# Block queries, keys and values in step-major scratch: one load each per step, input rows as 128 runs, two buffers shared

## The chip, the cores and the metric

The kernel runs on one core of a Trainium2 chip. A core has a matmul engine (TensorE, PE in the profile, with its weight loads as PEld), a vector engine (VectorE, DVE), a scalar engine (ScalarE, ACT), GpSimd (POOL) and a queue processor for transfers (SyncE, SP). Transfers are issued from the queues of SP, ACT and POOL and are carried out by 16 DMA engines that all queues share. The metric is the device time of one execution in microseconds (us). The kernel before took 2215.84 us, the median of three executions that lie between 2213.84 and 2217.09 us.

## The reference, cut to what matters

Two independent results are concatenated. The first (`A`) is a convolution over 2048 rows done by a Fourier transform. The second (`B`) is a recurrence over 64 segments, and most of the time goes there:

```python
# B: x (2048, 1024), 32 heads of 128, M = 8 memory rows, seg = 32
mem = mem0
for s in range(64):
    h = concatenate([mem, x[32 * s : 32 * s + 32]])        # 40 rows
    q, k, v = (einsum('td,dhe->hte', h, W) for W in (Wq, Wk, Wv))
    p = softmax(where(mask, q @ k.T * 128 ** -0.5, -1e9))  # a row sees the memory and earlier rows
    o = einsum('hte,hed->td', p @ v, Wo)
    mem = o[:8]
    outs.append(o[8:])
# A: outa = q * (causal_convolution(shift(k) * v, ssm_k) + ssm_D * shift(k) * v)
```

Each weight matrix is 1024 x 4096 in bf16, 8 MB. Four of them don't fit in the core's memory, so part of the weights is loaded again in every step.

## The kernel before, in words

**Stages.** Up to about 448 us the kernel computes `A` and, in between, prepares `B`. From then on it runs the recurrence, one step for each segment (`for s in range(n_seg)`, line 908), and after the last step it projects what was put aside, about 61 us.

**What is prepared.** Of the 40 rows of a step, the 8 memory rows and the first 24 rows of x go through the step's own projections. The last 8 rows of each segment, the *block rows*, depend on no memory: their queries, keys and values are computed for all 64 segments ahead of the recurrence, by the object `Rows` (lines 125 to 190). It works through 12 units, one for each projection (q, k, v) and group g of 8 heads, in the order q0 k0 v0 q1 k1 v1 v2 v3 q2 k2 q3 k3. Matmuls of such a unit stand between those of `A`; the accumulators are copied by ACT (from q3 on by ACT and DVE in turn) to the buffer `stq` (tile `st`, 128 x 64 x 128, queries and keys of a group) or `stv` (tile `sv`, 128 x 4 x 1024, values). Each of these has one buffer. When a group is complete, the whole tile is written to the scratch `QKBd` (line 184, after k0, k1, k2 and k3) or `VBd` (line 187, after v0 to v3), both from POOL's queue. The next unit of the kind can't write the buffer before that transfer has read it.

**A step.** It has four groups of 8 heads. For each group: the projections of queries and keys (`qk_part`, line 749), their copy to `qks` (`qk_out`, ACT), the value projection (`v_part`, 764) with its copy (`v_out`, ACT), transposes of `qks` (`tr_a`, PE) and copies of the result and of the block keys to QT and KT (DVE, 785 to 787). The scores, the softmax and the product with the values of group g are done among the projections of the next groups (`scores`, `softmax`, `pv`). After the fourth group come the output projections `wo` of all groups into Y, with the last softmax and products among them; ACT copies Y to `Y_sb` (961), PE transposes it, and DVE writes the memory rows into the next step's `hT` (`fill_mem`, 889). The next step's projections need that.

**Transfers of a step.** SP streams 17 pairs of weight tiles (512 KB each) through a ring of 5 buffers (`place`, 712): a load is issued when PE has finished with the ring slot. Between them SP issues four loads `qkb<-QKBd` (793), one for each group, each 128 rows of 256 bytes, into two buffers. POOL issues, at the end of a step, one store of block outputs (`OLd`, 856), four loads of the block values `VB` (798, 16 KB each) and four stores of the step's output from `Y_sb` (967). ACT issues one load of the next step's rows, `H` (661), at the start of group 2; `H` and `Y_sb` share one buffer (tag "st"), so this load waits for the four stores of the step before. `H` is transposed in `h_rows` (880) among the output projections.

**Order.** Instructions run on every engine in the order in which the program writes them. A wait of one instruction, a DMA issue too, holds everything behind it on the same queue. Transfers signal through a fixed set of semaphores, eight for those of SP and ACT together and eight for those of POOL, taken in turn: the ninth waits until the first has landed. So four stores, four loads and one store of a step on POOL's queue are one more than the eight.

**Names and lines of the steps to come:** `QKBd` 184 and 793, `VBd` 187 and 798, `load_h` 661, `h_rows` 880, `Y_sb` 961 and 967, `PT` (the transposed softmax, DVE, 834), the final loads of 512-byte rows 941.

## Time and profile before

| | us |
|---|---|
| median of three executions | 2215.84 |
| span of the profiled execution, first to last instruction | 2198.5 |
| median less span: what lies around the span (the page gives the profiled execution no other time of its own) | 17.3 |
| PE busy | 1808.6 (82%) |
| DVE busy | 1082.4 (49%) |
| ACT busy | 836.0 (38%) |
| POOL busy | 500.4 (23%) |
| first and last copy of Y to `Y_sb`: starts | 448.0 and 2137.0 |

A profile page gives busy times by engine, a picture of the span in 40 slices, the DMA queues with the packets that they moved (q1 is SP's, q10 ACT's, q0 POOL's, q8 fetches instructions), the chain of waits that ended last, and groups of instructions with what they waited for. The trace below it holds every packet with its size and its time on a DMA engine. The 64 copies to `Y_sb` mark the steps: 63 steps lie between 448.0 and 2137.0 us, 26.81 us each.

### The profile page before, as it was taken

Reading aid. Unit: us, or ns where it says so; the run is one execution under the profiler, and the core shown is the slowest. Engines: PE = TensorE matmul, PEld = TensorE weight load, DVE = VectorE, ACT = ScalarE, POOL = GpSimd, SP = SyncE. Lnnn points to the kernel's source line nnn. Section 1 sums busy time; section 2 is a strip of 40 time slices with the busy share of each in tenths; the row PEclk is TensorE's granted clock in tenths of the full one; section 3 lists DMA queues with packets and bytes.
Section 4 is the critical chain, followed back from the end, with each engine's and each line's share of the span. In section 5 each row is a group of like instructions: output and inputs, shape, how many; then the busy total and the mean of one; then the engine's idle time right before and its main releaser. Section 6 shows DMA issues by size and latency. Waiting matters only on the chain.

```text
span 2198.5 us, 88235 instructions
## 1 busy us (share of the span) xinstructions
PE 1808.6 (82%) x37779; PEld 1028.8 (47%) x37808; DVE 1082.4 (49%) x3235; ACT 836.0 (38%) x2538; POOL 500.4 (23%) x983
## 2 busy tenths in 40 slices
PE   4788877688888888788888878888888888888878
PEld 2332233354444445444544545544444445444558
DVE  6896822244544444444445445544444444444530
ACT  5456721133333334333333334333333333333320
POOL 4004622022222222222222222222222222222210
PEclk9999999899999999999999999999999999999999
DMA  7799889699999999999999999999999999999990
GB/s 255 267 353 350 302 302 369 248 354 345 343 341 365 344 358 367 339 342 333 349 352 361 365 357 364 364 345 353 358 353 347 349 347 361 323 348 345 357 328 21
DMA packets 275666, 732.29 MB, mean 333 GB/s; under 512 B 73323, under 2 KB 84539, under 8 KB 274761
## 3 DMA queue, kind: packets, MB, share of 16 engines
q1 hardware_dynamic: 242062, 683.06, 85.8%
q0 software_dynamic: 24320, 37.37, 5.2%
q10 hardware_dynamic: 8892, 6.23, 0.9%
q8 instruction: 295, 4.83, 0.9%
q14 instruction: 97, 0.79, 0.1%
HBM read 676.14 MB, written 59.18 MB: 334 GB/s over the span
## 4 chain that ended last, share of the span: by engine, by line
DMA 38%; PE 33%; issue 8%; DVE 3%; ACT 2%; POOL 1%; ACTq 1%; SPq 0%; POOLq 0%; DVEq 0%
PE qkacc L749 10%; DMA wring<-Wstv 10%; DMA wring<-Wstqk 8%; DMA wring<-Wsto 7%; PE yacc L863 6%; DMA out_dram<-Y_sb 5%; PE vacc L764 5%; DMA OLd<-OL 5%; PE otacc L846 3%; PE pl L979 3%; PE tp L777 2%; ACT OT L851 1%; PE otacc L848 1%; PE S L805 1%; DVE S L820 1%
## 5 line engine op out<-in xcount | busy, mean ns | idle before, releaser
L749 PE MATMUL qkacc<-Wqk,hT 128*32 128x512 bf16 x4096 | 354.6, 388 | 1.3 <-issue 1.3
L851 ACT CAST OT<-otacc 128x80 bf16<-128x80 f32 x1024 | 183.4, 233 | 438.6 <-PE otacc L848 391.2
L854 POOL COPY OL<-OT 128x64 bf16<-128x64 bf16 x252 | 63.3, 251 | 1221.9 <-ACT OT L851 1221.9
L764 PEld LDWEIGHTS <-hT 128*32 128x32 bf16 x8192 | 227.4, 98 | 190.1 <-issue 140.4
L749 PEld LDWEIGHTS <-hT 128*32 128x32 bf16 x8192 | 179.0, 98 | 215.4 <-issue 79.7
L863 PE MATMUL yacc<-Wo,OT 128*32 128x256 bf16 x5632 | 248.6, 278 | 22.2 <-issue 21.8
L863 PEld LDWEIGHTS <-OT 128*32 128x32 bf16 x8192 | 188.0, 97 | 103.5 <-issue 74.1
L764 PE MATMUL vacc<-Wv,hT 128*32 128x256 bf16 x5120 | 229.9, 279 | 2.7 <-issue 1.4
L749 PE MATMUL qkacc<-wring,hT 128*32 128x512 bf16 x2048 | 210.1, 398 | 24.3 <-DMA wring<-Wstqk 22.4
L764 PE MATMUL vacc<-wring,hT 128*32 128x256 bf16 x3072 | 145.4, 278 | 92.6 <-DMA wring<-Wstv 89.3
L846 PE MATMUL otacc<-PT,vsb 32*128 32x64 bf16 x2048 | 147.9, 192 | 55.3 <-ACT OT L851 49.1
L786 DVE COPY QT<-tp 128x256 bf16<-128x256 bf16 x256 | 74.7, 292 | 206.4 <-PE tp L777 198.8
L749 PE MATMUL qkacc<-Wearly,hT 128*32 128x512 bf16 x2048 | 171.0, 413 | 3.7 <-DVE hT L881 0.4
L718 ACT COPY wring<-park 128x1024 bf16<-128x1024 bf16 x128 | 129.9, 1015 | 110.4 <-PE qkacc L749 98.4
L755 ACT CAST qks<-qkacc 128x512 bf16<-128x512 f32 x256 | 150.5, 588 | 53.8 <-PE qkacc L749 48.6
L830 DVE TENSOR_REDUCE sm<-P 128x4 f32<-128x256 bf16 x256 | 107.6, 420 | 118.9 <-ACT P L828 118.9
L772 ACT CAST vsb<-vacc 128x256 bf16<-128x256 f32 x256 | 95.4, 373 | 179.2 <-PE vacc L764 178.2
L827 ACT ACTIVATE P<-S 128x128 bf16<-128x128 f32 x256 | 71.5, 279 | 238.3 <-DVE P L826 123.4
L819 DVE TENSOR_REDUCE mx<-S 128x4 f32<-128x160 f32 x256 | 83.2, 325 | 155.8 <-PE S L816 154.3
L863 PE MATMUL yacc<-wring,OT 128*32 128x256 bf16 x2520 | 131.5, 278 | 32.5 <-DMA wring<-Wsto 20.2
L798 POOL DMA_DIRECT2D VB<-VBd x256 | 152.3, 600 | 8.9 <-issue 3.6
L848 PE MATMUL otacc<-PT,VB 32*128 32x64 bf16 x2048 | 144.3, 188 | 8.9 <-issue 8.7
(218 smaller groups left out, 2830.0 us busy)
## 6 DMA issues: line engine op xcount, KB each, us to landing
wring<-Wstqk SPq DMA_DIRECT2D x448, 512.0 KB, 6.3
wring<-Wstv SPq DMA_DIRECT2D x320, 512.0 KB, 6.2
wring<-Wsto SPq DMA_DIRECT2D x315, 512.0 KB, 6.2
SK<-s_sb SPq DMA_DIRECT2D x8, 1024.0 KB
SU<-s_sb SPq DMA_DIRECT2D x8, 1024.0 KB, 5.4
QKBd<-stq POOLq DMA_DIRECT2D x4, 2048.0 KB, 9.8
Kg<-SK SPq DMA_DIRECT2D x16, 512.0 KB, 6.0
Ug<-SU SPq DMA_DIRECT2D x16, 512.0 KB, 8.0
```

The lines of the kernel that those rows point to most:

```text
L718: nc.scalar.copy(t[:, 0, :], park[key][0][:])
L749: nc.tensor.matmul(u.qk[p0:p0 + 32, :], lhsT=hT[:, kc, :], rhs=w[t][:, c2 * 512:(c2 + 1) * 512], start=(kc == 0), stop=(kc == 7), tile_pos ...
L755: nc.scalar.copy(u.qks[:], u.qk[:])
L764: nc.tensor.matmul(u.vacc[32 * c:32 * c + 32, 0:256], lhsT=hT[:, kc, :], rhs=w[kc % 2][:, c * 256:(c + 1) * 256], start=(kc == 0), stop=(k ...
L772: nc.scalar.copy(u.v[:], u.vacc[:, 0:256])
L798: nc.gpsimd.dma_start(VB[32 * c:32 * c + 32, :], VBd[8 * s:8 * s + 8].rearrange("r (g c x) -> c g r x", g=4, c=4)[c])
L819: nc.vector.tensor_reduce(out=mx[:], in_=S[:], op=ALU.max, axis=AX.X)
L830: nc.vector.tensor_reduce(out=sm[:], in_=P[:], op=ALU.add, axis=AX.X)
L846: nc.tensor.matmul(o, lhsT=u.v[r, i * 128:(i + 1) * 128], rhs=PTv[r, i, 0], start=True, stop=False, tile_position=(32 * c, 0))
L848: nc.tensor.matmul(o, lhsT=VB[r, i * 128:(i + 1) * 128], rhs=PTv[r, i, 1], start=False, stop=True, tile_position=(32 * c, 0))
L851: nc.scalar.copy(u.OT[:, 2 * c:2 * c + 2, :], ov[:, :, 0:40])
L863: nc.tensor.matmul(Y[32 * dq:32 * dq + 32, 0:256], lhsT=u.OT[:, hh, 0:32], rhs=w[hh % 2][:, dq * 256:(dq + 1) * 256], start=(u.g == 0 and ...
```

## The change

- The scratch `QKBd` is laid out by step: for a step, 128 rows of 4 groups x 128 values. A step loads it whole, 128 rows of 1 KB, in one transfer into one buffer, after the scores of the last group; `tr_a` and `scores` read slices of it. The price of the layout is on the writing side: a group's write has 128 x 64 runs of 256 bytes instead of 128 runs of 16 KB. It is issued from ACT's queue instead of POOL's.
- The scratch `VBd` is laid out so that a step's block values are one contiguous piece of 64 KB. One transfer loads it instead of four. A group's write is 16 transfers of 64 KB (runs of 512 bytes) on POOL's queue instead of one.
- The next step's input rows `H` are loaded as 128 rows of 512 bytes in the order of memory (partition = row x 4 + quarter), where the load before had the quarter outermost (4 x 32 x 512 bytes); `h_rows` reads its transposes in the new order. The first `H` takes two transfers instead of eight.
- `H` now shares its buffer with `qks`, and `Y_sb` with `PT`. The load of `H` is issued after the fourth group instead of before the third, `h_rows` stands after the last output projection, and the load of `VB` stands behind the four stores of `Y_sb`.

```diff
-    QKBd = dram.tile([4, 128, n_seg, 128], BF, name="QKBd")
+    QKBd = dram.tile([n_seg, 128, 4, 128], BF, name="QKBd")
-    VBd = dram.tile([n_seg * 8, 4096], BF, name="VBd")
+    VBd = dram.tile([n_seg, 4, 4, 8, 256], BF, name="VBd")
...
-                        nc.gpsimd.dma_start(QKBd[g].rearrange("e s x -> e (s x)"),
-                                            self.st[:].rearrange("e s h t r -> e (s h t r)"))
+                        nc.scalar.dma_start(QKBd[:, :, g, :].rearrange("s e x -> e s x"),
+                                            self.st[:].rearrange("e s h t r -> e s (h t r)"))
                     if m == "v" and j == 7:
-                        nc.gpsimd.dma_start(VBd.rearrange("(rb p) n -> p rb n", p=128)[:, :, g * 1024:(g + 1) * 1024],
-                                            self.sv[:])
+                        for rb_ in range(4):
+                            for c in range(4):
+                                nc.gpsimd.dma_start(VBd[16 * rb_:16 * rb_ + 16, c, g],
+                                                    self.sv[:, rb_, c * 256:(c + 1) * 256])
...
-        H_ = act.tile([128, 256], BF, tag="st", name="H")
+        H_ = act.tile([128, 256], BF, tag="qks", name="H")
...
-            nc.scalar.dma_start(H_[:], xq[:, 32 * s - 8:32 * s + 24, :])
+            nc.scalar.dma_start(H_[:], x[32 * s - 8:32 * s + 24].rearrange("t (dq c) -> (t dq) c", dq=4))
...
-    def load_b(s, g):
-        u = G()
-        u.g = g
-        u.qkb = act2.tile([128, 128], BF, tag="qkb", name="qkb")
-        nc.sync.dma_start(u.qkb[:], QKBd[g][:, s, :])
+    def load_b(s):
+        qkb = act.tile([128, 4, 128], BF, tag="qkb", name="qkb")
+        nc.sync.dma_start(qkb[:], QKBd[s])
+        return qkb
...
     def load_vb(s):
-        for c in range(4):
-            nc.gpsimd.dma_start(VB[32 * c:32 * c + 32, :],
-                                VBd[8 * s:8 * s + 8].rearrange("r (g c x) -> c g r x", g=4, c=4)[c])
+        nc.gpsimd.dma_start(VB[:], VBd[s].rearrange("c g r x -> (c g r) x"))
...
         for g in range(4):
-            if g == 2 and s + 1 < n_seg:
-                H = load_h(s + 1)
...
-            if g < 3:
-                nxt = load_b(s, g + 1)
-            elif s + 1 < n_seg:
-                nxt = load_b(s + 1, 0)
...
             v_out(u)
+            if g == 3 and s + 1 < n_seg:
+                H = load_h(s + 1)
...
-        softmax(us[3], scores(us[3]))
+        S = scores(us[3])
+        if s + 1 < n_seg:
+            qkb = load_b(s + 1)
+        softmax(us[3], S)
...
         wo(us[1], Y, range(4, 8))
+        wo(us[2], Y)
+        pv(us[3], s, (0, 1))
+        pv(us[3], s, (2, 3), True)
+        wo(us[3], Y)
         if s + 1 < n_seg:
             hT = new_hT()
             h_rows(H, hT, 8)
-        wo(us[2], Y)
-        pv(us[3], s, (0, 1))
-        pv(us[3], s, (2, 3), True)
-        if s + 1 < n_seg:
-            load_vb(s + 1)
-        wo(us[3], Y)
-        Y_sb = act.tile([128, 256], BF, tag="st", name="Y_sb")
+        Y_sb = act.tile([128, 256], BF, tag="PT", name="Y_sb")
...
         for dq in range(4):
             nc.gpsimd.dma_start(outb[32 * s:32 * s + 24, dq * 256:(dq + 1) * 256], Y_sb[32 * dq + 8:32 * dq + 32, :])
+        if s + 1 < n_seg:
+            load_vb(s + 1)
```

More of the change, by code (lines that the diff above doesn't have):

```diff
@@ L652, in load_h @@
     def load_h(s):
-        H_ = act.tile([128, 256], BF, tag="st", name="H")
-        xq = x.rearrange("t (dq c) -> dq t c", dq=4)
+        H_ = act.tile([128, 256], BF, tag="qks", name="H")
         if s == 0:
-            for dq in range(4):
-                nc.gpsimd.dma_start(H_[32 * dq:32 * dq + 8, :], mem0[:, dq * 256:(dq + 1) * 256])
-                nc.gpsimd.dma_start(H_[32 * dq + 8:32 * dq + 32, :], xq[dq, 0:24, :])
+            nc.gpsimd.dma_start(H_[0:32, :], mem0.rearrange("t (dq c) -> (t dq) c", dq=4))
+            nc.gpsimd.dma_start(H_[32:128, :], x[0:24].rearrange("t (dq c) -> (t dq) c", dq=4))
         else:
-            nc.scalar.dma_start(H_[:], xq[:, 32 * s - 8:32 * s + 24, :])
+            nc.scalar.dma_start(H_[:], x[32 * s - 8:32 * s + 24].rearrange("t (dq c) -> (t dq) c", dq=4))
         return H_
@@ L882, in h_rows @@
             hT_[:].rearrange("p (dq hf) t -> p dq hf t", hf=2)[:, :, :, r0:32],
-            tp[:, 0:256].rearrange("p (hf dq r) -> p dq hf r", hf=2, dq=4)[:, :, :, r0:32])
+            tp[:, 0:256].rearrange("p (hf r dq) -> p dq hf r", hf=2, dq=4)[:, :, :, r0:32])
     def fill_mem(hT_, Ysrc):
@@ L898, in fused_kernel @@
     load_vb(0)
-    nxt = load_b(0, 0)
+    qkb = load_b(0)
     for key in resident:
@@ L915, in fused_kernel @@
                     res[key] = res[at]
-            u = nxt
+            u = new_u(g)
             us.append(u)
```

6 lines of the change are left out of this document (4 added, 2 removed).

## The prediction

> **What bounds the kernel now.** I read the page first, then the stages by windows, then the waits inside the recurrence, then the places of the preparation that the change touches.
>
> ```profile
> PE 1808.6 (82%) x37779; PEld 1028.8 (47%) x37808; DVE 1082.4 (49%) x3235; ACT 836.0 (38%) x2538; POOL 500.4 (23%) x983
> DMA  7799889699999999999999999999999999999990
> q1 hardware_dynamic: 242062, 683.06, 85.8%
> q0 software_dynamic: 24320, 37.37, 5.2%
> q10 hardware_dynamic: 8892, 6.23, 0.9%
> ```
>
> The DMA row stands at 9 in nearly every slice, and SP's queue alone holds 85.8% of the time of 16 engines. The windows (columns: busy time of PE, PEld, DVE, ACT, POOL, granted clock, DMA share, GB/s) say where that is so:
>
> ```profile
> 187.00:250.00 63.00, 57.17 (x318) 17.86 (x321) 54.42 (x93) 48.83 (x92) 39.14 (x39) 1.00 1.00 356
> 250.00:285.00 35.00, 31.14 (x160) 9.56 (x163) 29.34 (x49) 25.89 (x49) 25.00 (x25) 1.00 0.66 228
> 361.00:373.00 12.00, 2.97 (x16) 1.30 (x15) 1.92 (x2) 0.59 (x1) 1.00 (x2) 0.78 0.98 394
> 385.00:402.00 17.00, 16.95 (x86) 7.95 (x85) 3.46 (x5) 2.85 (x5) 0.00 (x0) 1.00 0.35 125
> 402.00:414.00 12.00, 6.80 (x136) 3.55 (x135) 5.09 (x14) 5.09 (x9) 2.92 (x5) 1.00 0.48 182
> 600.00:2000.00 1400.00, 1173.78 (x28825) 687.83 (x28818) 672.65 (x2300) 525.17 (x1833) 313.73 (x681) 0.97 0.98 351
> ```
>
> In the recurrence (the last row) the DMA engines are full (0.98; 0.975 by the sum of the packets) and PE is not (1174 of 1400). Transfers bind it, and a step of 26.81 us has about 0.65 us of DMA idleness. The preparation changes its limit: PE with DVE and ACT in lockstep at 250 to 285, transfers at 361 to 373, PE at 385 to 402, and a single transfer at 402 to 414. What causes the idleness in the recurrence is in the waits there (total us, times, longest):
>
> ```profile
> SPq L793 <- DMA H<-in_B_x_dram: 86.1, 38, 5.1
> ACT OT L851 <- DMA out_dram<-Y_sb: 32.6, 10, 4.5
> POOL out_dram L967 <- DMA OLd<-OL: 53.4, 46, 3.1
> ```
>
> They are one string. POOL's ninth transfer of the step, the fourth output store, waits for the first (`OLd`). The load of `H` waits on ACT's queue for that store, because they share a buffer, and holds the copies behind it. SP's `qkb` load waits for `H`, whose semaphore it takes over, and the weight loads stand behind SP's `qkb`.
>
> **The change in the recurrence.** The trace's packet records give prices by size: 18.3 ns for 256 bytes (26,880 of them between 600 and 2000 us, all `qkb`), 29.3 ns for the 512-byte rows of `H`, 48.3 ns for 1 KB, 177 ns for 4 KB, 9.4 ns for a semaphore.
>
> - `qkb`: 4 x 128 x 18.3 / 16 = 0.586 us of every engine per step, against 128 x 48.3 / 16 = 0.386 (the 1 KB price is that of POOL's output stores). Three transfers fewer on SP, three on POOL: 6 x 9.4 ns. Sum -0.25 us a step, on the engines that bind: 63 x 0.25 = -16 us.
> - `VB`: the records show four packets of 4 KB for each 16 KB load, 16 a step; the single load moves the same bytes, so nothing but the semaphores. It saves POOL 3 x 0.58 us of issuing, on an engine with 314 of 1400 us busy. It now stands behind the four stores: Y's copy + 0.4, stores 4 x 0.52, own issue 0.6, landing 5.3, so about 8.4 us after the copy. The first user (the products of group 0, in group 2) comes about 11 us after it: hidden.
> - `H`: same bytes, but in the records (four steps after 1000 us) its 128 packets are never more than five at a time and take 2.0 to 4.8 us: about four of the sixteen engines carry it, 0.94 us each, instead of 0.23 on all. Spread evenly, the four lose 0.7 us a step. It is issued after the fourth group and needs 3.0 to 5.3 us; `h_rows` comes about 9 us later (1060 to 1069 us in one step of the chain). The transposes then run while ACT copies Y (0.37 us against 0.33): hidden.
> - The string of waits goes: six transfers on POOL's queue instead of nine, and `H` waits only for transposes just done. What is late next is `PT`: DVE's first transpose of a step must wait for the stores from `Y_sb`. In the trace it starts 7.9 to 10.8 us (median 9.3) after Y's copy; the last store would land at 0.4 + 3 x 0.52 + 5.1 = 7.1 us (longest 9.0). Mostly in time. If late, DVE's copies of QT and KT queue behind it and PE waits for these; the ring's lead covers part.
> - SP's `qkb` waits for the scores of group 3; the weight load behind it waits for a projection that PE does later anyway, so it holds up nothing. It is needed after the next `hT` (1061 to 1070 us in that step), against 5.2 us to land.
>
> How much of the 0.65 us of idleness goes is bounded by 0 (PE's own waits cause it) and 0.65 (41 us in all). The string costs SP 1.7 us a step, the uneven `H` 0.7 us on four engines; I take 0.3 us, just under half, -19 us. **Recurrence: -35 us**, between -16 and -57.
>
> **The change in the preparation.** No store of 256-byte runs is in the trace. Its nearest row is the 256-byte load, 18.3 ns; from below it can't be cheaper than its bytes at the 16 KB price (640 ns per 16 KB, 10 ns per 256 bytes); from above I take twice the load's, 36.6 ns, a row that is read before it is written. I take 18.3, since the prices above grow evenly with size whatever the kind: 8192 x 18.3 / 16 = 9.4 us per write against 128 x 640 / 16 = 5.1. The places where the writes stand, from the timeline of POOL, the waits of ACT, the chain, and the timeline of SP at the end (start, length):
>
> ```profile
> 187.18 0.56 POOL L184 DMA_DIRECT2D QKBd<-stq  x1
> 236.32 0.80 POOL L187 DMA_DIRECT2D VBd<-stv  x1 [0.38 <-ACT stv L149]
> 238.19 1.17 POOL L572 TENSOR_TENSOR Yre<-pa,pb 128x512 bf16<-128x512 bf16 x1
> ACT stq L149 <- DMA QKBd<-stq: 12.2, 1, 12.2
> 404.45 8.49 DMA QKBd<-stq
> 2120.89 11.58 SPq L941 DMA_DIRECT2D Wearly<-OLd  x2
> 2122.16 10.32 SPq L941 DMA_DIRECT2D Wearly<-OLd  x1
> ```
>
> - Writes after k0 (113 us) and k1 (187 us): +4.3 us of DMA each in full stretches, but loads run two sets ahead and 250 to 285 has DMA to spare. The issue moves from POOL to ACT, which at 187 us is in lockstep with PE (49 of 63 us busy), so what the issue takes there is lost. Of the final 512-byte loads, two on SP, the first (4096 runs) issues in 1.3 us, the second stands 10.3 us. For 8192 runs I take 3 us, ends 0.6 and 10. Sum +4 (0 to 13).
> - v0's 16 stores: POOL is idle. v1's at 236 us: 16 x 0.55 to 0.8 us, plus waits for semaphores, 10 us in which POOL's `Yre` and `Yim` are held up; PE uses them about 3 us later, so +7; ACT's copy to `stv` waits until the last lands, 236.3 + 10 + 5.3 = 251.6 against 242.8, 8.8 us, the same time over. +8 (5 to 12). v2's fall where POOL is free from 287 to 307. v3's at 316 us hold the stores of `A`'s output by 10 us; DVE waits for these stores already, but transfers bind there: +3 (0 to 9).
> - After k2 (361 us): the next unit's copy already waits 12.2 us for this write, and PE with it; 4.3 us more reach the end, since PE binds at 385 to 402: +4.5 (0 to 14).
> - After k3: the chain stands 2.37 us before POOL's issue and 8.49 for the landing (413.07). From ACT at 402.2: 1 + 9.4 + 1.2 gives 414: +1 (0 to 10). SP's `qkb` now waits for this write, but SP's loads of Wo behind it already did.
>
> **Preparation: +20.5 us.** Moving the write from POOL takes nothing off a path; its cover, idle POOL time, is exchanged for ACT's.
>
> **Sum.** Span 2198.5 - 35 + 20.5 = 2184; with the 17.3 us around it, 2201.3. The profiled execution's whole time isn't shown; I add the median's rest.
>
> **A rule against the change.** The Trainium skill's page "DMA: Bandwidth & Descriptors", section Specifications, puts line rate at 512 bytes and up and says that below it a DMA reads, modifies and writes. By that the 256-byte runs, harmless as loads, would cost double as stores, which is the rival "dear stores" below. No store of this trace can show it. The same page (section "Why a DMA increments its semaphore by 16 and not by 1") derives the number of engines from the outermost sizes; for `H` before, 4 and 128, that gives four, and the five at most in flight agree.
>
> **The rivals.**
>
> - *Dear stores*: each 256-byte run 36.6 ns. k2's and k3's writes add 9.4 us each to the path, the first two about 6 together: 2201 + 24.5 = 2226, slower. It decides from about 29 ns on: 24.5 us for 18.3 ns is 1.34 us per ns, and 10.8 ns more use up the gain of 14.5. For it: nothing in the trace writes short runs, and the steps of 128 KB between a partition's runs are new. Against: loads grow smoothly down to 256 bytes.
> - *ACT held by its own issue*, as SP's second load was: 10 us instead of 3 at 187 us, some 5 at 113: about 2213, no change. For: 512 runs an engine, twice what SP had queued in the first load. Against: the first load itself was taken at once.
> - *Idleness stays*: PE's waits, not the string, empty the queues: -16 + 20.5, 2220, slightly slower. For: SP waits more for PE (226 us on `qkacc`) than for `H`.
> - *All idleness goes*: -57 + 20.5, 2179.
>
> **How the numbers follow.** My forecast 0.45 (own range 2188 to 2211); all idleness 0.08; ACT held 0.12; idleness stays 0.13; dear stores 0.22. A change under 0.2% (4.4 us) can't be told from none here. Faster 0.45 + 0.08 = 0.53; same 0.12; slower 0.13 + 0.22 = 0.35. The range leaves out the edge of the best case and the worst of dear stores with a held ACT: 2176 to 2242.
>
> **What would show it.** Steps (63 between first and last copy of Y) near 26.25 us, with neither SP waiting for `H` nor ACT for `Y_sb`'s stores; the first copy of Y near 468 us instead of 448; 256-byte stores near 18 ns and four writes on q10. Wrong if ACT's issue at about 190 us lasts over 5 us, if k2's or k3's write takes 15 us or more, or if DVE's `PT` waits for the stores in many steps.

## The result, and the profile after

The changed kernel took 2188.57 us (median of 13 executions, 2183.43 to 2202.34). The kernel before, run beside it on the same chips, took 2210.56 (13 executions). The ratio is 0.9921, with a 95% interval of 0.9899 to 0.9943: 0.8% faster, where 2201 us and "faster" with a chance of 0.53 were forecast. The profiled spans, 2198.5 and 2186.4 us, differ by 12.1. The profiled execution of the kernel before lies below its median: in the 13 executions of the changed kernel the time is 1.8 to 2.4 us above the span, so by an estimate from these it took about 2200.6 us, 10 us less than the median of 2210.56. The profile doesn't show where the other executions spend these 10 us; if it is in the recurrence, a step of theirs is 0.16 us longer than the table's 26.81.

That net figure hides two larger ones. The first and the last copy of Y to `Y_sb` divide the span into preparation, recurrence and end:

| | before, us | after, us | difference | forecast |
|---|---|---|---|---|
| first copy of Y (preparation) | 447.96 | 486.67 | +38.7 | +20.5 |
| 63 steps between first and last copy | 1689.0 | 1638.4 | -50.6 | -35 |
| one step | 26.81 | 26.01 | -0.80 | -0.56 |
| from the last copy to the end of the span | 61.5 | 61.3 | -0.2 | 0 |
| span | 2198.5 | 2186.4 | -12.1 | -14.5 |

Both halves are larger than forecast by nearly the same amount (18 us and 16 us), so the sum came out nearly right although its two terms did not: that is luck.

The page of the changed kernel: busy time by engine, the DMA row in 40 slices, and the queues (packets, MB, share of 16 engines' time).

```profile
PE 1791.2 (82%) x37808; PEld 1023.5 (47%) x37808; DVE 1093.1 (50%) x3235; ACT 836.3 (38%) x2538; POOL 405.5 (19%) x841
DMA  7798969789999999999999999999999999999990
q1 hardware_dynamic: 214414, 683.05, 84.9%
q0 software_dynamic: 18368, 28.88, 4.0%
q10 hardware_dynamic: 42480, 14.62, 2.7%
```

The writes of block queries and keys now show as 42,480 packets on ACT's queue (q10, 8,892 before). SP's packets fall by 27,648: 384 rows and three transfers' semaphores on 16 engines fewer in each of 64 steps. POOL's busy time falls by 95 us. The DMA row still stands at 9 through the recurrence: the bound has not moved. The window over the recurrence (columns: busy time of PE, PEld, DVE, ACT, POOL, granted clock, DMA share, GB/s) shows the same:

```profile
600.00:2000.00 1400.00, 1185.83 (x29773) 703.17 (x29769) 706.64 (x2383) 543.43 (x1897) 222.85 (x541) 0.98 0.98 362
```

In the same 1400 us the engines carry 362 GB/s, where it was 351. What SP waits for inside the recurrence (us in total, times, longest):

```profile
SPq L712 <- PE qkacc L749: 318.3, 323, 3.9
SPq L712 <- DMA wring<-Wstqk: 250.0, 264, 4.1
SPq L712 <- PE yacc L865: 147.5, 142, 3.0
...
SPq L791 <- PE yacc L865: 59.7, 48, 3.1
```

The wait of 86.1 us for `H` is gone, as is ACT's wait for the output stores. SP waits instead for PE to free a ring slot (318 us, 226 before): the loads now arrive at the ring before PE is done with it. The load of the block queries and keys (line 791) waits for PE 48 times, and that was expected.

In the preparation the new writes stand out. The tile `QKBd` (issue min/median/max in ns, then the engines that waited for it):

```profile
L184 ACTq DMA_DIRECT2D QKBd<-stq x4: 366/372/389, 112.1 to 439.5; - x4
...
  ACT stq L149: 16.6, 1
  DVE stq L151: 11.0, 1
```

and the two waits of SP's queue in the windows from 105 to 150 us and from 197 to 230 us:

```profile
SPq L112 <- DMA QKBd<-stq: 12.5, 1, 12.5
...
SPq L520 <- DMA QKBd<-stq: 10.1, 1, 10.1
```

ACT issues such a write in 0.37 us, so ACT is not held by its issue. But the write lands late (a median of 16.5 us from issue to landing, 9.8 when the runs were 16 KB), and SP, which takes its semaphores from the same eight as ACT, twice stands behind it for over 10 us in the middle of `A`.

### The profile page after: what moved, and what is told of

Read it like the earlier page. It is cut to its first block, busy times and chain, and to the rows that moved or that the text cites. A ratio compares the mean times of both kernels' runs of the same rounds, so it can differ in the third digit from the quotient of the medians.

```text
span 2186.4 us, 88021 instructions
## 1 busy us (share of the span) xinstructions
PE 1791.2 (82%) x37808; PEld 1023.5 (47%) x37808; DVE 1093.1 (50%) x3235; ACT 836.3 (38%) x2538; POOL 405.5 (19%) x841
## 3 DMA queue, kind: packets, MB, share of 16 engines
q10 hardware_dynamic: 42480, 14.62, 2.7%
## 4 chain that ended last, share of the span: by engine, by line
PE 45%; DMA 34%; DVE 8%; issue 7%; ACT 5%; POOL 1%; SPq 0%; ACTq 0%; DVEq 0%; POOLq 0%
PE qkacc L749 13%; DMA wring<-Wstv 13%; DMA wring<-Wstqk 10%; PE yacc L865 8%; PE vacc L764 5%; PE otacc L848 3%; PE pl L980 3%; DMA wring<-Wsto 2%; DMA QKBd<-stq 2%; PE tp L777 2%; PE ps_k L176 1%; PE S L807 1%; DVE S L822 1%; DVE mx L821 1%; PE ps_q L176 1%
## 5 line engine op out<-in xcount | busy, mean ns | idle before, releaser
L764 PEld LDWEIGHTS <-hT 128*32 128x32 bf16 x8192 | 220.2, 97 | 181.5 <-issue 103.3
L749 PEld LDWEIGHTS <-hT 128*32 128x32 bf16 x8192 | 178.1, 97 | 216.4 <-issue 77.0
L865 PEld LDWEIGHTS <-OT 128*32 128x32 bf16 x8192 | 194.6, 97 | 84.9 <-issue 61.4
L850 PE MATMUL otacc<-PT,VB 32*128 32x64 bf16 x2048 | 141.4, 188 | 10.8 <-issue 10.8
L966 POOL DMA_DIRECT2D out_dram<-Y_sb x256 | 129.2, 511 | 38.1 <-ACT Y_sb L960 35.0
## 6 DMA issues: line engine op xcount, KB each, us to landing
QKBd<-stq ACTq DMA_DIRECT2D x4, 2048.0 KB, 16.5
```

The costliest lines, as they stand in the source:

```text
L749: nc.tensor.matmul(u.qk[p0:p0 + 32, :], lhsT=hT[:, kc, :], rhs=w[t][:, c2 * 512:(c2 + 1) * 512], start=(kc == 0), stop=(kc == 7), tile_pos ...
L764: nc.tensor.matmul(u.vacc[32 * c:32 * c + 32, 0:256], lhsT=hT[:, kc, :], rhs=w[kc % 2][:, c * 256:(c + 1) * 256], start=(kc == 0), stop=(k ...
L850: nc.tensor.matmul(o, lhsT=VB[r, i * 128:(i + 1) * 128], rhs=PTv[r, i, 1], start=False, stop=True, tile_position=(32 * c, 0))
L865: nc.tensor.matmul(Y[32 * dq:32 * dq + 32, 0:256], lhsT=u.OT[:, hh, 0:32], rhs=w[hh % 2][:, dq * 256:(dq + 1) * 256], start=(u.g == 0 and ...
L966: nc.gpsimd.dma_start(outb[32 * s:32 * s + 24, dq * 256:(dq + 1) * 256], Y_sb[32 * dq + 8:32 * dq + 32, :])
```

## The experiments

The questions: which part of the change shortens the step, which part lengthens the preparation, and whether the three supposed mechanisms (the string of waits, the short runs, the uneven `H`) are the ones at work. "Step" below is the distance between the first and the last copy of Y divided by 63; "idle" and "work" are the parts of it in which the DMA engines stood still or moved packets (from the packet records); "4 KB" is the mean time of a weight packet. "First Y" is the length of the preparation. The kernel before of each ratio ran beside it. Each step comes from one profiled execution, and the executions of one kernel differ by up to 28 us (four_2pool, 2198.75 to 2226.71), which is 0.44 us a step if all of it lies in the recurrence; so differences of a few hundredths of a us say nothing by themselves, and larger ones are trusted where the medians agree.

| kernel | median, us | ratio, 95% interval | first Y | step | idle | work | 4 KB, ns |
|---|---|---|---|---|---|---|---|
| before | 2210.56 | | 448.0 | 26.81 | 0.65 | 26.16 | 176.9 |
| after | 2188.57 | 0.9921 (0.9899 to 0.9943) | 486.7 | 26.01 | 0.45 | 25.55 | 174.5 |
| h_late | 2167.13 | 0.9797 (0.9741 to 0.9852) | 447.4 | 26.31 | 0.38 | 25.93 | 174.9 |
| one_load | 2161.70 | 0.9828 (0.9757 to 0.9900) | 451.0 | 26.08 | 0.23 | 25.85 | 174.8 |
| h_quarter | 2186.61 | 0.9889 (0.9833 to 0.9945) | 483.1 | 26.04 | 0.36 | 25.68 | 175.1 |
| four_vb | 2189.66 | 0.9918 (0.9886 to 0.9949) | 483.1 | 26.06 | 0.48 | 25.57 | 174.1 |
| four_loads | 2258.86 | 1.0214 (1.0151 to 1.0277) | 487.3 | 27.25 | 0.92 | 26.33 | 178.9 |
| qkb_write | 2225.87 | 1.0110 (1.0046 to 1.0174) | 465.5 | 26.96 | 0.73 | 26.24 | 177.4 |
| qk_pool | 2194.05 | 0.9958 (0.9910 to 1.0005) | 489.2 | 26.15 | 0.49 | 25.65 | 175.1 |
| v_spread | 2168.07 | 0.9839 (0.9770 to 0.9908) | 471.5 | 25.97 | 0.39 | 25.58 | 174.9 |
| two_loads | 2194.99 | 0.9937 (0.9900 to 0.9974) | 484.2 | 26.15 | 0.52 | 25.63 | 174.7 |
| four_spaced | 2232.74 | 1.0104 (1.0072 to 1.0136) | 487.1 | 26.61 | 0.62 | 25.99 | 176.4 |
| four_h_pool | 2229.90 | 1.0112 (1.0078 to 1.0145) | 487.2 | 26.64 | 0.76 | 25.88 | 176.0 |
| four_2pool | 2216.65 | 1.0014 (0.9978 to 1.0049) | 490.0 | 26.43 | 0.55 | 25.88 | 176.3 |

### The recurrence, part by part

**The string of waits alone (h_late).** The kernel before with only the buffers of `H` and the place of its load and transposes changed; no scratch layout is touched, and the four short loads a step stay.

```diff
-        H_ = act.tile([128, 256], BF, tag="st", name="H")
+        H_ = act.tile([128, 256], BF, tag="qks", name="H")
...
-            if g == 2 and s + 1 < n_seg:
-                H = load_h(s + 1)
...
+            if g == 3 and s + 1 < n_seg:
+                H = load_h(s + 1)
...
-        if s + 1 < n_seg:
-            hT = new_hT()
-            h_rows(H, hT, 8)
         wo(us[2], Y)
...
         wo(us[3], Y)
+        if s + 1 < n_seg:
+            hT = new_hT()
+            h_rows(H, hT, 8)
```

> The kernel before with one part done alone: H shares its buffer with qks instead of Y_sb, is loaded after the fourth group, and h_rows stands after the last output projection. Scratch, qkb loads, VB and the quarter-outermost H stay as before. If the string of waits (H behind the stores, SP's qkb behind H) emptied the queues, SP's wait for H (86 us between 600 and 2000 us) and ACT's wait for the stores (33 us) go and the step falls from 26.81 by 0.2 to 0.5 us (13 to 32 us, 2178 to 2198 where the kernel before has 2210). If PE's own waits empty them, the step stays within 0.1 us of 26.8.

Measured: 26.31 us a step, 0.50 less than before, and the preparation as it was; 2167 us. Of the 0.80 us that the whole change saves per step, 0.50 come from this edit. SP's waits in its recurrence no longer hold line 793 behind `H`:

```profile
SPq L712 <- PE qkacc L749: 257.6, 261, 3.3
SPq L712 <- PE yacc L863: 187.5, 175, 3.3
...
SPq L712 <- DMA H<-in_B_x_dram: 52.0, 26, 4.5
```

A wait for `H` is left, but on loads of weights, in 26 steps instead of 38, and 52 us instead of 86. ACT no longer waits for the output stores. PE now waits 13 times, 22.2 us in all, for `H` itself (line 880, 600 to 2000 us), which it doesn't in the changed kernel. The idle time falls by 0.27 us a step, and the weight packets become shorter, 176.9 to 174.9 ns, which over some 136 of them per engine and step is the other half.

**One load, without the 1 KB rows (one_load).** The changed kernel's loop on the scratch layouts and the writes of the kernel before: a step's block queries and keys come in one transfer, but as 512 rows of 256 bytes, and `VB` in four transfers.

```diff
-    QKBd = dram.tile([n_seg, 128, 4, 128], BF, name="QKBd")
+    QKBd = dram.tile([4, 128, n_seg, 128], BF, name="QKBd")
-    VBd = dram.tile([n_seg, 4, 4, 8, 256], BF, name="VBd")
+    VBd = dram.tile([n_seg * 8, 4096], BF, name="VBd")
...
-                        nc.scalar.dma_start(QKBd[:, :, g, :].rearrange("s e x -> e s x"),
-                                            self.st[:].rearrange("e s h t r -> e s (h t r)"))
+                        nc.gpsimd.dma_start(QKBd[g].rearrange("e s x -> e (s x)"),
+                                            self.st[:].rearrange("e s h t r -> e (s h t r)"))
...
-        nc.sync.dma_start(qkb[:], QKBd[s])
+        nc.sync.dma_start(qkb[:], QKBd[:, :, s, :].rearrange("g e x -> e g x"))
...
```

> The changed kernel's recurrence on the scratch layouts of the kernel before: QKBd by group and VBd by row, written as before by POOL in whole runs, and a step's queries and keys in one transfer of 4 x 128 rows of 256 bytes; VB in four transfers; H, the shared buffers and the order as in the changed kernel. If the preparation's 39 us come from the new layouts, the first copy of Y is back at 448 to 452 us. If only the 256-byte packets distinguish the recurrence, the step is 26.01 + 0.2 = 26.2 us, 2150 to 2170 in all, 1.9% under the kernel before. If what made four loads cost 1.24 us a step was the size of their runs and not their number, the step is near 27.2 and the time near 2220.

Measured: 26.08 us a step, 0.07 more than after, and the preparation only 3 us longer than before: 2162 us, 27 us under the changed kernel's median. The short rows do cost packet time (work 25.85 against 25.55), yet the step hardly shows it: the engines stand idle 0.23 us instead of 0.45. So the 1 KB rows are worth about 0.07 us a step, some 4 us in all, no more than the executions of one kernel differ, and for them and the single load of `VB` the layouts pay some 36 us in the preparation (486.7 against 451.0).

**H with the quarter outermost (h_quarter).** The changed kernel with the old order of `H`'s rows (4 x 32 x 512 bytes).

```diff
+        xq = x.rearrange("t (dq c) -> dq t c", dq=4)
...
-            nc.scalar.dma_start(H_[:], x[32 * s - 8:32 * s + 24].rearrange("t (dq c) -> (t dq) c", dq=4))
+            nc.scalar.dma_start(H_[:], xq[:, 32 * s - 8:32 * s + 24, :])
...
-            tp[:, 0:256].rearrange("p (hf r dq) -> p dq hf r", hf=2, dq=4)[:, :, :, r0:32])
+            tp[:, 0:256].rearrange("p (hf dq r) -> p dq hf r", hf=2, dq=4)[:, :, :, r0:32])
```

> The changed kernel with one part undone: H is loaded with the quarter outermost again (4 x 32 x 512 bytes, about four of the sixteen engines), and h_rows reads its transposes in that order. Everything else stays, so H still waits for nothing but transposes. The measure is the step, the mean distance of the 63 copies to Y_sb: 26.01 us in the changed kernel, 26.81 before. If the uneven load cost time (four engines with 0.94 us instead of 0.23 each step), the step grows by 0.3 to 0.7 us (19 to 44 us in all, 2207 to 2232 against 2188). If only the string of waits cost time, the step stays within 0.1 us of 26.0.

Measured: 26.04 us a step against 26.01, and the intervals of the ratios overlap: no effect. The 0.7 us on four engines, real in the packet records, did not reach the step's end.

**VB in four transfers (four_vb).**

```diff
-        nc.gpsimd.dma_start(VB[:], VBd[s].rearrange("c g r x -> (c g r) x"))
+        for c in range(4):
+            nc.gpsimd.dma_start(VB[32 * c:32 * c + 32, :], VBd[s, c])
```

> The changed kernel with the one transfer of VB undone: four transfers of 32 x 512 bytes behind the four stores, so POOL's queue has nine transfers a step again. My theory (the string of waits needed H behind the stores) has the step within 0.1 us of 26.01. The rival, that small transfers of POOL stretch the weight packets (177 ns before, 174.6 after in the recurrence), has it at 26.2 or more and the 4 KB packets of SP's queue back at 176 ns or above.

Measured: 26.06 us a step, 2189.66 us: no effect, as the hidden issue of POOL made likely.

**Four short loads again (four_loads).** The changed kernel with the step's block queries and keys in four transfers of 128 x 256 bytes, back to back.

```diff
-        nc.sync.dma_start(qkb[:], QKBd[s])
+        for g in range(4):
+            nc.sync.dma_start(qkb[:, g, :], QKBd[s, :, g, :])
```

> The changed kernel with the 1 KB rows undone in the recurrence alone: the new scratch and its writes stay, but a step loads its block queries and keys in four transfers of 128 x 256 bytes into the slices of the one buffer. By the prices of the packets the step grows by 0.2 us of DMA work and three semaphores, 0.23 us in all, 26.01 to 26.24 (14 us, about 2203). If SP's issue and the semaphores that three more transfers take weigh as well, it grows by 0.5 us or more. If the four loads are hidden, it stays within 0.1 us.

Measured: 27.25 us a step, 1.24 more than with one load, and slower than the kernel before. The same 512 rows of 256 bytes in *one* transfer cost 0.07 (one_load). So it is neither the size of the rows nor their packets but the number of transfers. From its waits in the recurrence, of SP:

```profile
SPq L712 <- DMA H<-in_B_x_dram: 59.9, 48, 2.3
```

In nearly every step a load of weights waits for `H`, which it doesn't read: it takes over the semaphore. One step of SP's timeline (start, length):

```profile
1070.07 1.59 SPq L712 DMA_DIRECT2D wring<-Wsto  x2
1072.85 2.44 SPq L792 DMA_DIRECT2D qkb<-QKBd  x4
1075.38 0.85 SPq L712 DMA_DIRECT2D wring<-Wstqk  x2
1077.68 0.80 SPq L712 DMA_DIRECT2D wring<-Wstv  x2
```

`H` was issued by ACT at 1071.9 and took 5.7 us to land, until 1077.6. Behind it go four `qkb` and two `Wstqk`; then SP stands, and the two `Wstv` start at 1077.68, just when `H` has landed. SP and ACT share eight semaphores (their transfers carry the numbers 100, 102 to 107 and 109 in the trace, those of POOL 111 to 118), so eight transfers are the most that they can have open, and the ring alone wants five.

### Is it the number of open transfers?

Four runs put this to a test: two loads of 512-byte rows (two_loads); the four loads apart from each other (four_spaced); the four loads with `H` on POOL's queue, which has semaphores of its own (four_h_pool); and the same with the fourth load on POOL's queue too (four_2pool).

two_loads:

```diff
-        nc.sync.dma_start(qkb[:], QKBd[s])
+        for gp in range(2):
+            nc.sync.dma_start(qkb[:, 2 * gp:2 * gp + 2, :], QKBd[s, :, 2 * gp:2 * gp + 2, :])
```

> The changed kernel with the block queries and keys of a step loaded by two adjacent transfers of 128 x 512 bytes instead of one of 128 x 1 KB. Theory A (semaphores held by a burst): with two of eight held instead of one, a cost well under a third of the 1.24 us of four loads, since five or six stay for the ring of five: 26.0 to 26.3 us a step, about 2190 to 2205 us. Theory B (a cost for each transfer, 1.24 / 3 = 0.41 us): 26.4 us a step, about 2214 us. Packets alone: 256 x 29.3 / 16 = 0.469 us against 0.386, so at least 0.08 more than 26.01.

four_spaced (`load_b` loads the groups that it is given):

```diff
-            qkb = load_b(s + 1)
+            qkb = load_b(s + 1, (0,))
         softmax(us[3], S)
         wo(us[0], Y, range(4, 8))
+        if s + 1 < n_seg:
+            load_b(s + 1, (1,), qkb)
         pv(us[2], s, (0, 1))
         wo(us[1], Y, range(0, 4))
+        if s + 1 < n_seg:
+            load_b(s + 1, (2,), qkb)
         pv(us[2], s, (2, 3))
         wo(us[1], Y, range(4, 8))
+        if s + 1 < n_seg:
+            load_b(s + 1, (3,), qkb)
```

> The changed kernel with the block queries and keys of a step loaded by four transfers of 128 x 256 bytes again, from the new layout, but apart from each other: one after the scores of group 3, the others after the second quarter, the third quarter and the fourth of the first eight output projections, so that loads of weights stand between them on SP's queue. The same four loads back to back took 27.25 us a step against 26.01 with one load. Theory A (the burst does it: four adjacent short loads take four of the eight semaphores of SP and ACT at once and leave the ring of weights fewer transfers in flight): most of the 1.24 us goes; what stays is the packets' own time (0.2) and the semaphores: 26.2 to 26.4 us a step, about 2205 us. Theory B (the number or the short rows themselves cost it, wherever they stand): 27.0 to 27.3 us a step, about 2250 us. The first copy of Y near 485 us in both.

four_h_pool, against four_loads:

```diff
-            nc.scalar.dma_start(H_[:], x[32 * s - 8:32 * s + 24].rearrange("t (dq c) -> (t dq) c", dq=4))
+            nc.gpsimd.dma_start(H_[:], x[32 * s - 8:32 * s + 24].rearrange("t (dq c) -> (t dq) c", dq=4))
```

> The four adjacent loads of the block queries and keys, with the next step's rows H loaded from POOL's queue (own semaphores) instead of ACT's. Theory A, sharpened: SP and ACT together have eight transfers open at most; the ring of weights wants five of them, H one, the block queries and keys one, two or four. 7 open (one load): 26.01 us a step; 8 (two loads): 26.15; 10 (four loads): 27.25, of which the packets' own time is 0.2. With H elsewhere it is 9 and SP's wait for H (60 us in the four adjacent loads, on the loads of weights) is gone: clearly below 27.25, 26.5 to 27.0 us a step, 2215 to 2245 us. Theory B (four short transfers cost it, whatever semaphores they take): 27.2 to 27.3 us a step, 2255 to 2265 us.

four_2pool, against four_h_pool:

```diff
-            nc.sync.dma_start(qkb[:, g, :], QKBd[s, :, g, :])
+            by = nc.gpsimd if g == 3 else nc.sync
+            by.dma_start(qkb[:, g, :], QKBd[s, :, g, :])
```

> As the last, and the fourth of the four loads of the block queries and keys from POOL's queue too, so that SP has at most 5 + 3 = 8 transfers open and POOL 8 a step. The same packets go through the same 16 engines. Theory A: as with two loads, 26.15, and the 0.15 to 0.2 us of the short packets: 26.2 to 26.5 us a step, 2195 to 2215 us. Theory B: 27.0 to 27.3 us a step, 2245 to 2265 us. A third outcome, POOL's load late because POOL waits for ACT ahead of it, would show as DVE's KT copy waiting for qkb in many steps.

What these runs gave, ordered by the step. The third column is counted from the traces, which name the semaphore of each wait: the time between 600 and 2000 us in which SP stood at the very semaphore that its next transfer takes, so until an earlier transfer with that semaphore had landed.

| kernel | open on SP and ACT at once (ring + `H` + `qkb`) | SP's wait for its next transfer's semaphore, us | step, us |
|---|---|---|---|
| after | 5 + 1 + 1 = 7 | 0.3 | 26.01 |
| one_load | 5 + 1 + 1 = 7 | 0.3 | 26.08 |
| two_loads | 5 + 1 + 2 = 8 | 13.4 | 26.15 |
| four_2pool | 5 + 0 + 3 = 8 | 19.7 | 26.43 |
| four_spaced | 5 + 1 + up to 4, a little apart | 80.0 | 26.61 |
| four_h_pool | 5 + 0 + 4 = 9 | 50.3 | 26.64 |
| four_loads | 5 + 1 + 4 = 10 | 98.7 | 27.25 |

The step grows with the transfers that SP and ACT want open, and moving two of four_loads' transfers to POOL's queue, with the same bytes on the same 16 engines, takes 0.82 of the 1.24 us away. The medians in the first table agree (four_loads 2258.86, four_2pool 2216.65, after 2188.57 us). The theory that four short transfers cost it wherever their semaphores lie (27.0 to 27.3 in all three runs) falls. The wait in the third column grows with the step too, but for four_spaced. It bounds what the semaphores cost from above, since the ring slot that the transfer needs may not have been free either. By the same count it is 112.9 us in the kernel before, most of it the wait of `qkb` for `H`, and 51.3 in h_late. So the whole change takes this wait from 112.9 to 0.3 us, and h_late alone a little over half of it.

The steps of three runs lie within what the semaphores led to expect. The fourth, four_spaced, doesn't quite: 26.2 to 26.4 was expected and 26.61 measured. In its trace the loads stand hardly apart: they start 0.8 to 1.0 us after one another (medians; 0.4 to 0.5 when adjacent) and take some 5 us to land, so that all four are still open together, and half of the cost is left. In h_late they start 3.7 to 6.7 us apart. A load of weights still waits for `H` in 47 of the 52 or 53 steps of this stretch (48 in four_loads).

```profile
SPq L712 <- DMA H<-in_B_x_dram: 53.4, 47, 2.2
```

With `H` on POOL's queue (four_h_pool) SP never waits for `H`, and for a `qkb` load five times, 3.8 us in all; the rest of its 50.3 us it stands at semaphores that earlier loads of weights hold. What stays open is the rest of four_2pool against two_loads, 0.28 us: 0.2 to 0.25 of it is the longer work of its packets (25.88 against 25.63), but one_load moves rows of the same size with work of 25.85 and loses nothing by it.

### The preparation, part by part

**The layout of block queries and keys alone (qkb_write).** The kernel before with the new layout of `QKBd` and its writes from ACT; the loads stay four a step.

```diff
-    QKBd = dram.tile([4, 128, n_seg, 128], BF, name="QKBd")
+    QKBd = dram.tile([n_seg, 128, 4, 128], BF, name="QKBd")
...
-                        nc.gpsimd.dma_start(QKBd[g].rearrange("e s x -> e (s x)"),
-                                            self.st[:].rearrange("e s h t r -> e (s h t r)"))
+                        nc.scalar.dma_start(QKBd[:, :, g, :].rearrange("s e x -> e s x"),
+                                            self.st[:].rearrange("e s h t r -> e s (h t r)"))
...
-        nc.sync.dma_start(u.qkb[:], QKBd[g][:, s, :])
+        nc.sync.dma_start(u.qkb[:], QKBd[s, :, g, :])
```

> The kernel before with only the new layout of QKBd and its writes from ACT; a step still has four spaced loads of 128 x 256 bytes, two buffers, the old H, VB and order. The step should stay at 26.8 us, and the first copy of Y come later than 448 us by what these writes cost alone. By the changed kernel's milestones that is 11.7 (k0) + 6.2 (k1) + 5.5 (k2) + 1 (k3) = 24 us: first copy at 472, total about 2235 where the kernel before has 2211. By the packets' work alone (4.3 us of DMA each, half of it hidden) it would be 456 and 2219.

Measured: first Y at 465.5, 17.5 us later than before, between the 456 and the 472 that were expected, and by itself a loss: 1.1% slower. By difference, the other 21 us of the changed kernel's 38.7 belong to the writes of block values.

**The same writes from POOL's queue (qk_pool).**

```diff
-                        nc.scalar.dma_start(QKBd[:, :, g, :].rearrange("s e x -> e s x"),
+                        nc.gpsimd.dma_start(QKBd[:, :, g, :].rearrange("s e x -> e s x"),
```

> The changed kernel with the four writes of QKBd issued from POOL's queue instead of ACT's; layout and runs of 256 bytes stay. SP shares its semaphores with ACT, not with POOL: in the changed kernel SP's loads stood 12.5 us (at 121 us) and 10.1 us (at 208 us) for such a write. If these waits are the cost of the first two writes, the first copy of Y falls from 487 us to 465 to 475. If the many short runs themselves cost the time (the same packets on the same engines), it stays at 480 or more; it rises if POOL needs long to describe 8192 runs, which holds up Yre and Yim.

Measured: SP no longer waits for these writes, and `Yre` starts at 185.7 us instead of 191.3 (before: 180.8). Yet the first Y is no earlier, 489.2: POOL needs 2.8 us to issue what ACT issues in 0.37, and after k3 nothing hides it: from the start of ACT's last copy of the rows to the first Y it is 53.4 us, against 49.7 in the changed kernel. Of the 5 us lead at the end of `Yre` 1.2 us are left at the last output store; what takes the rest in between no run divides.

```profile
L184 POOL DMA_DIRECT2D QKBd<-stq x4: 2781/2793/2806, 112.3 to 439.8; - x4
```

So SP's waits of 12.5 and 10.1 us are worth 5 to 6 us of the preparation, not all of the slip; the theory that they are the main part falls.

**The stores of block values spread over the unit (v_spread).** The changed kernel with two of the 16 stores after each of the eight copies to `stv`, instead of all 16 after the last.

```diff
-                    if m == "v" and j == 7:
-                        for rb_ in range(4):
-                            for c in range(4):
-                                nc.gpsimd.dma_start(VBd[16 * rb_:16 * rb_ + 16, c, g],
-                                                    self.sv[:, rb_, c * 256:(c + 1) * 256])
+                    if m == "v":
+                        for c in (2 * (j % 2), 2 * (j % 2) + 1):
+                            nc.gpsimd.dma_start(VBd[16 * rb:16 * rb + 16, c, g],
+                                                self.sv[:, rb, c * 256:(c + 1) * 256])
```

> The changed kernel with the 16 stores of a group of values spread over the unit: two after each copy to stv instead of all sixteen behind the last. Bytes, runs and queue stay. If POOL's sixteen issues in a row and the copies that wait for them cost the 9 us after v1 (252 to 264 us) and some 4 us after v3, the first copy of Y falls from 487 us by 8 to 13. If the number of transfers costs it wherever they stand, it stays within 3 us.

Measured: first Y at 471.5, 15.2 us earlier than after, with the same step (25.97); 2168 us. The 64 stores therefore cost some 21 us in a block and some 6 spread out. POOL's timeline of the *changed* kernel shows the block after v1 (start, length, idle before and what ended it):

```profile
252.72 5.86 POOL L189 DMA_DIRECT2D VBd<-stv  x11
260.50 1.10 POOL L189 DMA_DIRECT2D VBd<-stv  x2 [1.92 <-DMA VBd<-stv]
261.99 0.53 POOL L189 DMA_DIRECT2D VBd<-stv  x1 [0.39 <-DMA VBd<-stv]
262.78 1.05 POOL L189 DMA_DIRECT2D VBd<-stv  x2 [0.26 <-issue]
263.82 1.07 POOL L121 DMA_DIRECT2D Wstv<-in_B_Wv_dram  x2
264.90 1.16 POOL L574 TENSOR_TENSOR Yre<-pa,pb 128x512 bf16<-128x512 bf16 x1
```

For 11 us POOL issues stores and computes no `Yre`, and it waits twice for one of its own earlier stores to land (1.92 and 0.39 us). In v_spread two stores stand between two `Yre` steps, in 1.05 us, where POOL was waiting for DVE anyway:

```profile
248.88 1.16 POOL L573 TENSOR_TENSOR Yre<-pa,pb 128x512 bf16<-128x512 bf16 x1 [0.69 <-DVE pb L570]
250.42 1.05 POOL L188 DMA_DIRECT2D VBd<-stv  x2 [0.38 <-ACT stv L149]
251.96 1.16 POOL L573 TENSOR_TENSOR Yre<-pa,pb 128x512 bf16<-128x512 bf16 x1 [0.48 <-DVE pb L570]
```

### A version that beats both

one_load (2161.70 us), h_late (2167.13) and v_spread (2168.07) beat the kernel before by 1.6 to 2%, and their medians are 20 us or more under the changed kernel's. h_late's interval (up to 0.9852) lies clear of the changed kernel's (from 0.9899); those of one_load (up to 0.9900) and v_spread (up to 0.9908) just reach it. Which of the three is the fastest isn't shown. one_load and h_late need no new scratch layout.

## Why the prediction was right, and where it was not

**The bound and the string of waits: right in kind, too small in size.** The recurrence was read as bound by transfers, with one string of waits from POOL's ninth transfer through `H` to SP's `qkb`. h_late removes that string and gains 0.50 us a step. What the string did is told by the semaphores: SP's 86.1 us at `H` are the larger part of the 112.9 us for which it stood at its next transfer's semaphore, and in the changed kernel 0.3 us of these are left. The term "how much of the 0.65 us of idleness goes" was set at 0.3, between 0 and 0.65. In the changed kernel the idle time fell by just 0.19 (0.65 to 0.45). What the sum had no term for is that the weight packets become shorter as well, 176.9 to 174.5 ns: their records on SP's queue fall from 24.02 to 23.71 us a step. The upper bound of -57 held (-50.6 measured).

**The packets (-0.25 us a step, -16 us): right as records, wrong as a cause.** The records fall by what was worked out: `qkb` from 0.583 to 0.398 us (0.586 to 0.386 forecast), the semaphores by 0.05. But one_load keeps the short rows and loses 0.07. Work that goes away turned into idle time there (0.45 against 0.23 us). What fewer transfers on SP bring is the semaphores that they no longer hold, which the prediction priced as packets of 9.4 ns each: four adjacent transfers, instead of one, cost 1.24 us a step. The kernel before had its four apart, one for each group, and paid far less: h_late, with four apart and the string gone, stands at 26.31, just 0.23 above one_load. How much of these 0.23 us is the loads isn't shown: the two kernels also differ in the order of `H`, in the buffer of `Y_sb` and in the place of `VB`'s load, and PE's 22.2 us of waits for `H` in h_late are 0.42 us a step.

**The uneven `H`: a cost that wasn't there.** Counted as a part of the idleness (0.7 us on four engines). h_quarter restores it at no loss. In the Trainium skill's page "DMA: Bandwidth & Descriptors", section "Why a DMA increments its semaphore by 16 and not by 1", the number of engines follows from the outermost sizes; the records of before agree with that for the most part (in the time in which packets of `H` move, more than four do so at once in 2%, in the changed kernel in 8%), but no time hung on it here.

**`PT` behind the stores: right.** "Mostly in time" held; in the changed kernel's recurrence no `PT` waits for the stores from `Y_sb`. `VB` late behind the stores: hidden, as forecast; four_vb changes nothing.

**The preparation (+20.5 us): +38.7, the term that was mis-sized.** By places, from the start and end of `Yre`, the last store of `A`'s output, the last copy of the rows and the first Y (before and after, with qkb_write to divide them):

| step of the prediction | forecast | measured |
|---|---|---|
| writes after k0 and k1 | +4 (0 to 13) | +13.2 (qkb_write, end of `Yre` 282.9 to 296.1) |
| stores after v0 and v1 | +8 (5 to 12) | +12.9 (end of `Yre` 309.0, less qkb_write's 296.1) |
| stores after v2 and v3 | +3 (0 to 9) | about +5 (last output 365.8 to 397.0, less the 26.1 up to `Yre`'s end) |
| write after k2 | +4.5 (0 to 14) | +4.3 |
| write after k3 | +1 (0 to 10) | +3.2 |

The step that failed is the first. It put the cost into ACT's issue ("I take 3 us"), which took 0.37; and it let the DMA time of the two writes, 4.3 us each, vanish in "loads run two sets ahead". It followed the semaphores of SP and ACT in the recurrence but not here: SP's loads for `A` stood behind k0's and k1's writes for 12.5 and 10.1 us (worth 5 to 6 us by qk_pool). The rest of the 13.2 is not divided by any run, so its cause stays open; the write's landing of 19.95 us in the full stretch at 198 us is the likely place. The second, v1's stores, was right in mechanism: 16 issues took 11.1 us of POOL (10 forecast), but 8 us of it were to be lost once; with v0 it was 12.9.

After k2 the step holds in detail: the next unit's copy waited 16.6 us for the write (12.2 before), 4.4 more, where 4.3 was worked out. One of the prediction's signs of being wrong came in here all the same: k2's write took 16.5 us from issue to landing, more than 15. The sign was set too tight, since 10.8 us before and the 4.3 worked out are 15.1 already.

For k3 the prediction read the trace wrongly: it let ACT issue the write from 402.2 us on. But the copies of this unit go to ACT and DVE in turn, and the last, DVE's, ends at 403.9; POOL issued the write at 404.45, so there was only half a us to gain. In the changed kernel ACT issues it 0.07 us after that copy, the write lands after 11.2 us instead of 8.5, and +3.2 is measured where +1 was forecast.

**The rivals.** *Dear stores* is out: 256-byte stores took 18.9 ns in the mean of 32,768 packet records (18.3 taken, 36.6 the rival). The rule that the prediction cites from the Trainium skill's page "DMA: Bandwidth & Descriptors", section Specifications, that a transfer below 512 bytes reads, modifies and writes, shows no price in these stores beside the loads of the same size. *ACT held by its own issue* is out at 0.37 us. *Idleness stays* is out by h_late. *All idleness goes* didn't happen in the changed kernel (0.45 us left), but one_load comes down to 0.23.

**The sum.** Two errors of opposite sign, +18.2 us in the preparation and -15.6 in the recurrence, nearly cancel: the span was forecast at 2184 and measured at 2186.4. That they cancel is luck, and so in part is the sign. With the preparation as measured and the recurrence as forecast the span would have grown by 3.7 us (38.7 - 35). The reason given, the string of waits, is worth 31.5 us by h_late (63 x 0.50), less than the 38.7 us that the preparation pays; the rest of the gain came with the other parts of the change. The forecast of 2201.3 us lies 12.7 above the measured 2188.6 because of another term, the 17.3 us of "median less span" that were added. That rest isn't a constant: in the changed kernel it is 2.2 us, in four_loads it is -6.4, since one profiled execution is set against the median of others. The range held.

## What to carry to other kernels

Count the transfers that one set of semaphores must hold open at once, on all queues that share it, before counting bytes: here a ring of five and eight semaphores left room for three more, and with nine or ten wanted the step grew by 0.6 and 1.2 us, more than the packets' own work. Removing a wait that ran through three queues (a shared buffer) brought most of the gain for a few moved lines, while a layout that made the reads ideal moved its price to the writes, where little of it was hidden. And a block of 16 small stores on an engine that also computes should be spread between its computations.

## What the runs showed of the hardware that was not expected

- Short stores are hardly dearer than short loads: 18.9 ns for a 256-byte store from ACT's queue, 18.1 to 18.4 ns for a load from SP's, each from thousands of packets.
- The issue of the same transfer of 8192 runs took 0.37 us from ACT's queue and 2.79 us from POOL's (qk_pool).
- The mean time of a 4 KB packet is not constant: 174.1 to 175.1 ns with up to 0.52 us of idle time a step, 176.0 to 177.4 ns with 0.55 to 0.76, 178.9 ns with 0.92. Between the ends, 4.8 ns on 136 packets of an engine are 0.65 us a step, as much as the whole idle time of the kernel before. Why the packets are longer when the engines are less full isn't shown by any run here.
